# Attention feeding an MLP on one core: weights fetched earlier, less work in the first phase, and the last stores on two queues

## The chip, the core and the metric

The kernel runs on one core of a Trainium2 chip. The core has TensorE (matrix products, written to the accumulation memory PSUM), VectorE, ScalarE and GpSimd (elementwise work), and 16 DMA engines that move data between the chip's memory and the on-chip memory SBUF. SyncE (SP in the profile) issues nearly all DMAs here. The metric is the device time of one execution in microseconds, lower is better.

## The reference

Eight batches of eight heads of attention, with a head dimension of 64. 512 local queries attend to the keys at most 32 positions away and to 32 global keys; 32 global queries attend to all 544 keys. The result, 8 x 544 = 4352 rows of 512, goes through an MLP with a hidden width of 2048.

```python
s_g = scale * q_g @ k_all.T;  out_g = softmax(s_g) @ v_all
s_ll = where(|i - j| <= 32, scale * q_l @ k_l.T, -1e9);  s_lg = scale * q_l @ k_g.T
out_l = softmax(concat(s_lg, s_ll)) @ concat(v_g, v_l)
x = concat(out_g, out_l).transpose(0, 2, 1, 3).reshape(4352, 512)
h = x @ w_in;  out = (h * sigmoid(h)) @ w_out
```

## The kernel before

**Two jobs, one stream of TensorE work.** The attention runs in 128 steps, k = 0 to 127: batch b, a tile c of 128 query rows, a pair of heads pr. Four steps make a tile of x, and 34 tiles (32 local ones, 2 that gather the global queries) make the MLP's 12 blocks: ten of three tiles, two of two (`SIZES`). The first phase is the attention of block 0, steps 0 to 11, with the scores of steps 12 and 13. Then the MLP runs block by block, each with 16 slices f of the hidden width: `first_layer` makes h (12 matmuls), ScalarE and VectorE make gh and gl of it, and `second_layer` adds nine matmuls into the block's outputs (a value is carried as a rounded part and a rest, so each product is three). While block n runs, `fill` slips the attention of block n + 1 between its matmuls.

**A step.** `st_load` fetches raw (queries and keys), `st_scores` makes the scores on TensorE (L357), adds mask and maximum on VectorE (L364), takes the exponential on ScalarE (L368), and scales both halves by the reciprocal of the sum (L372 on ScalarE, L376 on VectorE; for k from 12 to 27 the second is on ScalarE too). `st_turn` transposes the result on TensorE for k below 12 (L404, copied by ScalarE at L406), later steps go over `st_halves` (GpSimd), `st_away` and `st_back` (two DMAs). `st_out` multiplies by v (L437); for k = 4 to 11 it first issues `WARMS[2]` matmuls of zeros into the same bank. The global queries have loads of their own (`g_load`, L234), scores (L259) and a softmax.

**Weights.** A slice f of the weights comes in two halves, w_in's and w_out's, as 8-byte numbers. `fetch_weights(f, half)` issues the DMA of one half (512 KB, L198) into a home that is free by then; `join_weights` makes 4-byte numbers of one half, in order (ScalarE L214, VectorE L216 and L217); `split_weights(f)` makes the rounded part and the rest of a whole slice (ScalarE L226, VectorE L227). In block 0, before slice f, the loop at the end splits slice f + 1, joins up to slice f + 2, and fetches what is not yet fetched of (f + 5, 0) and the half that goes with it.

**Who sets the order.** Everything in the attention is put on a list with a time in units of steps (`put`), and the list, sorted, is the program. `FIRSTW` says how many half slices are fetched at which step, `JOINS` and `SPLITS` at which times the first slices are joined and split. DMAs on SP, the weights' operations and the masks are kept in program order; TensorE's order is the program's; the other instructions of ScalarE and VectorE are ordered by a planner when the program is built. A load that needs a buffer waits on SP until the buffer's last reader is done, and what is queued behind it waits too: raw has two buffers after step 8.

**The end.** After the last block's last slice, ScalarE scales each output tile (L627) and the stores go out: the last block's second tile holds the global rows of four batches and has four stores, on SP; its first tile has one, on ScalarE's queue.

Of the kernel before, what the change touches and what calls it, by code (L numbers as in the profile page):

```python
# [9 lines left out]
F32 = mybir.dt.float32  # L10
# [5 lines left out]
AF = mybir.ActivationFunctionType  # L16
ALU = mybir.AluOpType
# [4 lines left out]
P = 128  # L22
# [3 lines left out]
W = 224  # L26
HALO = 32
SKV = SG + SL
DM, DFF = H * D, 2048
# [9 lines left out]
SIZES = (3,) * 10 + (2, 2)  # L39
# [4 lines left out]
KP = 12  # L44
WHOLE = 9
WARM = 288
WARMS = (14, 8, 3)
SINGLE = 12
SCRATCH = 8
FETCH, LOOK = 5, 3  # L50
PLACES = ("ws15", "ws14", "ws13", "klo", "ws14", "ws15", "klo", "qk")
FIRSTW = {4: 2, 5: 2, 6: 1, 7: 1, 8: 1, 9: 1, 10: 1, 11: 1}
JOINS, SPLITS = (9.0, 9.6, 10.2, 10.8, 11.4, 12.0), (12.1, 12.7)

FIRST = dict(load=(-1.2, -1.1, -1.0, 0.1), vload=(1.22, 1.23, 2.22, 2.23), turn=(3.2, 4.0, 4.9, 5.8), out=(4.3, 5.2, 6.1, 7.0),
             gload=(1.2, 1.21, 2.2, 2.21), gscores=(3.4, 4.2, 5.1, 6.0), gsoft=(4.4, 6.2), gturn=(6.9, 8.0),
             late=8.5, then=7.3)
# [12 lines left out]
def attention_moe_kernel(ctx: ExitStack, tc: tile.TileContext, qk0_in, qk_in, v_in, gqk, wts, out):  # L70
# [274 lines left out]
    def st_scores(k, b, c, pr):  # L345
        if k < ND:
            raw = tiles.pop(("raw", k))
        else:
            qk, klo = tiles.pop(("qk", k))
        s = attbank("s", f"s{k}")  # L350
        if k == 0:
            warm(s, WARMS[0])
        ss = [s[:, u * W : (u + 1) * W] for u in range(2)]
        for u in range(2):
            qs, ks = slice(u * P, (u + 1) * P), slice(u * W, (u + 1) * W)
            if k < ND:
                nc.tensor.matmul(ss[u], raw[:, qs], raw[:, QW : QW + W], start=True, stop=True)  # L357
            else:
                nc.tensor.matmul(ss[u], qk[:, qs], qk[:, QW:][:, ks], start=True, stop=False)  # L359
                nc.tensor.matmul(ss[u], qk[:, qs], klo[:, ks], start=False, stop=True)  # L360
        p = probs_tile(k)
        st = small.tile([P, 8], F32, tag="st", name=f"st{k}")
        for u in range(2):
            nc.vector.tensor_tensor_reduce(out=p[:, u, :W], in0=ss[u], in1=mask_of[c],  # L364
                                           scale=-SCALE, scalar=3.0e38, op0=ALU.add, op1=ALU.min,
                                           accum_out=st[:, u : u + 1])
        for u in range(2):
            nc.scalar.activation(p[:, u, :W], p[:, u, :W], AF.Exp, bias=st[:, u : u + 1], scale=-1.0,  # L368
                                 accum_out=st[:, 2 + u : 3 + u])
        nc.vector.tensor_scalar(out=st[:, 4:6], in0=st[:, 2:4], scalar1=1e-9, scalar2=None, op0=ALU.add)  # L370
        nc.vector.reciprocal(out=st[:, 6:8], in_=st[:, 4:6])  # L371
        nc.scalar.activation(p[:, 0, :W], p[:, 0, :W], AF.Copy, scale=st[:, 6:7])  # L372
        if KF <= k < ND:
            nc.scalar.activation(p[:, 1, :W], p[:, 1, :W], AF.Copy, scale=st[:, 7:8])
        else:
            nc.vector.tensor_scalar(out=p[:, 1, :W], in0=p[:, 1, :W], scalar1=st[:, 7:8], scalar2=None,  # L376
                                    op0=ALU.mult)
        tiles["p", k] = p.rearrange("p u j -> p (u j)")
# [113 lines left out]
    def put(when, fn, *a):  # L492
        stream.append((when, fn, a))

    AHEAD = NPR
    for k, (t, b, c, pr) in enumerate(steps):
        a = (k, b, c, pr)
        j = k % NST
        due = dict(DUE)
        if k >= KF:  # L500
            due.update(DMAT)
            due.update({} if pr else DMAT0)
        if k < AHEAD:
            due.update({part: FIRST[part][k] - k for part in ("load", "vload", "turn", "out")})
        elif pr == 0:
            due["vload"] = VLOADS[min(k // NPR, 3)]
        if k == AHEAD:
            for h in range(NPR):
                put(FIRST["gload"][h], g_load, 0, h)
                put(FIRST["gscores"][h], g_scores, 0, h)  # L510
            for hh in range(2):
                put(FIRST["gsoft"][hh], g_soft, 0, hh)
                put(FIRST["gturn"][hh], g_turn, 0, hh)
            put(FIRST["late"], g_late)
            at = FIRST["then"]
            for when in JOINS:
                put(at + when - NPR, join_weights)
            for f, when in enumerate(SPLITS):
                put(at + when - NPR, split_weights, f)
        if j == 0 and b:  # L520
            for hh in range(2):
                put(at + (TURN if b > 1 else TURN1)[hh], g_turn, b, hh)
        for i in range(FIRSTW.get(k, 0)):
            put(at + 0.01, fetch_weights, *divmod(sum(FIRSTW.get(j, 0) for j in range(k)) + i, 2))
        put(at + due["load"], st_load, *a)
        put(at + due["split"], st_split, *a)
        put(at, st_scores, *a)
        if "vload" in due:
            put(at + due["vload"], st_vload, *a)
        if k >= KF:  # L530
            put(at + due["halves"], st_halves, *a)
            put(at + due["away"], st_away, *a)
        put(at + due["turn"], st_turn, *a)
        if k >= KF:
            put(at + due["back"], st_back, *a)
        if k < SINGLE or pr == NPR - 1:
            n = 1 if k < SINGLE else NPR
            put(at + due["out"], st_out, k - n + 1, n, b, c, t)
            marks[t] = at + due["out"]
        if j == NST - 1 and b % 4 == 3:  # L540
            put(marks[t] + 0.001, g_tile, t + 1)
            marks[t + 1] = marks[t] + 0.001
        if b + 1 < B:
            first, every = HEADS if b > 1 else HEADS0
            for h in [h for h in range(NPR) if first + h * every == j]:
                for part, fn in (("load", g_load), ("split", g_split), ("scores", g_scores)):
                    put(at + HEAD[part], fn, b + 1, h)
                if h % 2:
                    put(at + HEAD["soft"], g_soft, b + 1, h // 2)
                at += HEAD["slot"]  # L550
        at += 1.0
# [26 lines left out]
    def out_rows(t):  # L578
        kind, b, c = order[t]
        if kind == "l":  # L580
            return [(0, P, b * SKV + SG + c * P)]
        return [(SG * i, SG, (4 * b + i) * SKV) for i in range(4)]
# [22 lines left out]
    def second_layer(n, f, gh, gl):  # L605
# [14 lines left out]
            if done_ % 3 == 0:  # L620
                fill(1)
        if f == NF - 1:
            done_ = work.tile([P, 3 * DM], F32, tag=f"xh{n % 2}", name=f"o{n}")
            for i in (reversed(range(SIZES[n])) if last else range(SIZES[n])):
                o = outs[n][i]
                sb = done_[:, DM * i : DM * (i + 1)]
                nc.scalar.activation(sb, o, AF.Copy, scale=0.5)  # L627
                for p0, np_, r in out_rows(sum(SIZES[:n]) + i):
                    queue = nc.sync if n == 0 or last and i else nc.scalar
                    queue.dma_start(out=out[r : r + np_, :], in_=sb[p0 : p0 + np_, :])  # L630

    advance(ends[0])
    early.clear()
# [88 lines left out]
```

## Time and profile before

| | us |
|---|---|
| three runs | 975.33, 976.76, 976.23 (median 976.23) |
| the profiled execution | 976.78 |
| its span, first to last instruction | 974.9 |
| TensorE busy | 950.1 |
| VectorE, ScalarE, GpSimd busy | 624.1, 584.1, 201.7 |
| MLP's first matmul at | 48.17 |

The profile is of one execution. Its own time is longer than its span by what lies before the first and after the last instruction (1.88 us). Times in rows are counted from the span's start. PE is TensorE, PEld its weight loads, DVE VectorE, ACT ScalarE, POOL GpSimd, SPq and ACTq the issue of DMAs on SP and ScalarE. A busy time is a union of instructions, which overlap in the engine's pipeline; matmuls' ends are modelled. PEclk 1.00 is the full granted clock.

### The profile page before, as it was taken

Reading aid. Unit: us, or ns where it says so; the run is one execution under the profiler, and the core shown is the slowest. Engines: PE = TensorE matmul, PEld = TensorE weight load, DVE = VectorE, ACT = ScalarE, POOL = GpSimd, SP = SyncE. Lnnn points to the kernel's source line nnn. Section 1 sums busy time; section 2 is a strip of 40 time slices with the busy share of each in tenths; the row PEclk is TensorE's granted clock in tenths of the full one; section 3 lists DMA queues with packets and bytes.
Section 4 is the critical chain, followed back from the end, with each engine's and each line's share of the span. In section 5 each row is a group of like instructions: output and inputs, shape, how many; then the busy total and the mean of one; then the engine's idle time right before and its main releaser. Section 6 shows DMA issues by size and latency. Waiting matters only on the chain.

```text
span 974.9 us, 17433 instructions
## 1 busy us (share of the span) xinstructions
PE 950.1 (97%) x5790; PEld 847.1 (87%) x5790; DVE 624.1 (64%) x1884; ACT 584.1 (60%) x1494; POOL 201.7 (21%) x413
## 2 busy tenths in 40 slices
PE   7889999999999999999999999999999999999998
PEld 5678788898898989989899899989999899989897
DVE  4888976766676677656577567766677566453322
ACT  7978776656656556555566656665575655443332
POOL 2113222122222122112122222212222221120000
PEclk9999999999999999999999999999999999999999
DMA  8799956656575766534756576575666564433000
GB/s 268 244 275 300 288 158 170 179 158 184 160 169 158 198 156 175 167 98 104 188 146 167 148 211 178 137 201 145 169 192 158 154 163 142 126 91 82 1 23 22
DMA packets 189305, 157.32 MB, mean 161 GB/s; under 512 B 128672, under 2 KB 148640, under 8 KB 189216
## 3 DMA queue, kind: packets, MB, share of 16 engines
q1 hardware_dynamic: 184848, 148.35, 56.0%
q10 hardware_dynamic: 4368, 7.87, 2.3%
q8 instruction: 46, 0.75, 0.3%
q14 instruction: 43, 0.35, 0.1%
HBM read 86.44 MB, written 39.32 MB: 129 GB/s over the span
## 4 chain that ended last, share of the span: by engine, by line
PE 69%; DMA 3%; ACT 1%; DVE 1%; issue 1%; POOL 0%; SPq 0%; ACTq 0%; POOLq 0%; DVEq 0%
PE out L618 30%; PE h L591 29%; PE o L437 5%; PE s L359 2%; PE s L360 2%; DMA raw<-in_qk_dram 2%; DMA raw_g<-in_gqk_dram 1%; DMA away<-halves 0%; PE gs L268 0%; PE gt L305 0%; PE gs L269 0%; POOL halves L386 0%; ACT qk L341 0%; SPq L395 0%; DVE qk L343 0%
## 5 line engine op out<-in xcount | busy, mean ns | idle before, releaser
L386 POOL COPY halves<-probs 128x512 uint16<-128x512 uint16 x232 | 152.1, 682 | 490.7 <-ACT probs L372 186.9
L598 ACT ACTIVATE t<-h 128x384 f32<-128x384 f32 (+1 forms) x192 | 90.5, 472 | 160.0 <-PE h L591 145.0
L599 DVE SCALAR_TENSOR_TENSOR t<-t,h 128x384 f32<-128x384 f32 (+1 forms) x192 | 101.7, 529 | 108.1 <-ACT t L598 107.4
L618 PE MATMUL out<-w_hi,gh 128*128 128x512 f32 x544 | 164.8, 401 | 2.7 <-ACT gh L601 2.6
L591 PE MATMUL h<-xh,w_hi 128*128 128x384 f32 (+1 forms) x768 | 160.6, 330 | 4.7 <-ACT w_hi L226 4.0
L618 PE MATMUL out<-w_hi,gl 128*128 128x512 f32 x544 | 161.2, 395 | 0.2 <-DVE gl L602 0.2
L618 PE MATMUL out<-w_lo,gh 128*128 128x512 f32 x544 | 161.1, 394 | 0.0
L591 PE MATMUL h<-xl,w_hi 128*128 128x384 f32 (+1 forms) x768 | 158.2, 327 | 0.0
L591 PE MATMUL h<-xh,w_lo 128*128 128x384 f32 (+1 forms) x768 | 158.2, 327 | 0.0
L368 ACT ACTIVATE probs<-probs,st 128x224 f32<-128x224 f32 x244 | 115.9, 476 | 59.0 <-DVE st L364 58.1
L591 PEld LDWEIGHTS h<-xh,w_hi 128*128 128x128 f32 x768 | 132.7, 188 | 20.6 <-ACT w_hi L226 6.2
L602 DVE TENSOR_TENSOR gl<-t,gh 128x384 fp32r<-128x384 f32 (+1 forms) x192 | 109.6, 571 | 43.6 <-ACT gh L601 39.4
L364 DVE CUSTOM_DVE_ANT_0 probs<-s,mask 128x224 f32<-128x224 f32 x244 | 86.1, 387 | 74.9 <-PE s L360 63.2
L591 PEld LDWEIGHTS h<-xl,w_hi 128*128 128x128 f32 x768 | 132.7, 188 | 0.0
L591 PEld LDWEIGHTS h<-xh,w_lo 128*128 128x128 f32 x768 | 131.3, 188 | 0.3 <-DVE w_lo L227 0.2
L601 ACT CAST gh<-t 128x384 fp32r<-128x384 f32 (+1 forms) x192 | 94.4, 491 | 55.0 <-DVE t L599 54.7
L618 PEld LDWEIGHTS out<-w_hi,gl 128*128 128x128 f32 x544 | 100.3, 188 | 22.6 <-DVE gl L602 1.0
L618 PEld LDWEIGHTS out<-w_lo,gh 128*128 128x128 f32 x544 | 100.5, 188 | 21.6 <-issue 0.6
L618 PEld LDWEIGHTS out<-w_hi,gh 128*128 128x128 f32 x544 | 93.5, 189 | 14.8 <-ACT gh L601 5.6
L341 ACT CAST qk<-raw 128x704 fp32r<-128x704 f32 x100 | 77.7, 777 | 31.7 <-DMA raw<-in_qk_dram 27.8
L342 DVE TENSOR_TENSOR klo<-raw,qk 128x448 fp32r<-128x448 f32 x100 | 64.4, 644 | 34.1 <-ACT qk L341 31.6
L372 ACT ACTIVATE probs<-probs,st 128x224 f32<-128x224 f32 x122 | 58.6, 480 | 34.1 <-DVE st L371 32.2
(92 smaller groups left out, 1071.3 us busy)
## 6 DMA issues: line engine op xcount, KB each, us to landing
raw<-in_qk_dram SPq DMA_DIRECT2D x100, 352.0 KB, 3.4
away<-halves SPq DMA_DIRECT2D x116, 256.0 KB, 2.9
vraw<-in_v_dram SPq DMA_DIRECT2D x30, 512.0 KB, 4.7
raw_w<-in_wts_dram SPq DMA_DIRECT2D x29, 512.0 KB, 6.2
raw_g<-in_gqk_dram SPq DMA_DIRECT2D x32, 304.0 KB, 4.3
out_dram<-o ACTq DMA_DIRECT2D x29, 256.0 KB, 3.7
raw<-in_qk_dram SPq DMA_DIRECT2D x28, 240.0 KB, 4.5
pt<-away SPq DMA_TRANSPOSE x116, 3.3
```

What stands on the lines that cost most here:

```text
L341: nc.scalar.copy(out=qk, in_=raw)
L342: nc.vector.tensor_tensor(out=klo[:, :KW], in0=raw[:, QW:], in1=qk[:, QW:].bitcast(F32), op=ALU.subtract)
L364: nc.vector.tensor_tensor_reduce(out=p[:, u, :W], in0=ss[u], in1=mask_of[c], scale=-SCALE, scalar=3.0e38, op0=ALU.add, op1=ALU.min, accum_ ...
L368: nc.scalar.activation(p[:, u, :W], p[:, u, :W], AF.Exp, bias=st[:, u : u + 1], scale=-1.0, accum_out=st[:, 2 + u : 3 + u])
L372: nc.scalar.activation(p[:, 0, :W], p[:, 0, :W], AF.Copy, scale=st[:, 6:7])
L386: nc.gpsimd.tensor_copy(out=halves[:, :, u], in_=p[:, 2 * P * u : 2 * P * (u + 1)].bitcast(U16).rearrange("p (j h) -> p h j", h=2))
L591: nc.tensor.matmul(h[:, :nt], wt[:, c * P : (c + 1) * P], x[:, c, :nt], start=(i == 0), stop=(i == 3 * NCC - 1))
L598: nc.scalar.activation(t[:, :nt], h[:, :nt], AF.Tanh, scale=0.5)
L599: nc.vector.scalar_tensor_tensor(out=t[:, :nt], in0=t[:, :nt], scalar=1.0, in1=h[:, :nt], op0=ALU.add, op1=ALU.mult)
L601: nc.scalar.copy(out=gh[:, :nt], in_=t[:, :nt])
L602: nc.vector.tensor_tensor(out=gl[:, :nt], in0=t[:, :nt], in1=gh[:, :nt].bitcast(F32), op=ALU.subtract)
L618: nc.tensor.matmul(outs[n][i], g[:, i * P : (i + 1) * P], w, start=(f == 0 and j == 0), stop=(f == NF - 1 and j == 2))
```

## The change

1. Scaling of the first half (L372) for k below 8 (`LEAN`): VectorE instead of ScalarE.
2. One matmul of zeros instead of three ahead of the outputs of steps 4 to 11.
3. `FIRSTW` becomes a list of half slices by step, 18 instead of 10. Of the eight, (5, 0) and (5, 1) were the first that block 0 issued; the other six, (7, 0), (8, 1), (6, 1), (7, 1), (9, 1) and (10, 1), came in its slices f = 1 to 6. The sorted list puts them on SP thus: load of raw 9, (3, 0), (3, 1), raw 10, (4, 0), (4, 1), raw 11, (5, 0), (5, 1), (7, 0), first global load of batch 1, raw 12, (8, 1), (6, 1), (7, 1), second global load, raw 13, (9, 1), (10, 1), third global load, raw 14. Before it was raw 9, (3, 0), raw 10, (3, 1), raw 11, (4, 0), first global load, raw 12, (4, 1), second global load, raw 13, third, raw 14.
4. Four joins and two splits in the first phase instead of six and two; slice 2 is joined by the loop's first turn.
5. At the end the last tile's eviction is cut in two (ScalarE, VectorE), and the fourth store of the global rows goes on ScalarE's queue behind the store of the last tile.

```diff
@@ -44,13 +44,15 @@
 KP = 12
 WHOLE = 9
 WARM = 288
-WARMS = (14, 8, 3)
+WARMS = (14, 8, 1)
+LEAN = 8
 SINGLE = 12
 SCRATCH = 8
 FETCH, LOOK = 5, 3
 PLACES = ("ws15", "ws14", "ws13", "klo", "ws14", "ws15", "klo", "qk")
-FIRSTW = {4: 2, 5: 2, 6: 1, 7: 1, 8: 1, 9: 1, 10: 1, 11: 1}
-JOINS, SPLITS = (9.0, 9.6, 10.2, 10.8, 11.4, 12.0), (12.1, 12.7)
+FIRSTW = {4: ((0, 0), (0, 1)), 5: ((1, 0), (1, 1)), 6: ((2, 0),), 7: ((2, 1),), 8: ((3, 0), (3, 1)),
+          9: ((4, 0), (4, 1)), 10: ((5, 0), (5, 1), (7, 0)), 11: ((8, 1), (6, 1), (7, 1)), 12: ((9, 1), (10, 1))}
+JOINS, SPLITS = (9.0, 9.7, 10.4, 11.1), (11.8, 12.4)
 
 FIRST = dict(load=(-1.2, -1.1, -1.0, 0.1), vload=(1.22, 1.23, 2.22, 2.23), turn=(3.2, 4.0, 4.9, 5.8), out=(4.3, 5.2, 6.1, 7.0),
              gload=(1.2, 1.21, 2.2, 2.21), gscores=(3.4, 4.2, 5.1, 6.0), gsoft=(4.4, 6.2), gturn=(6.9, 8.0),
@@ -369,7 +371,10 @@
                                  accum_out=st[:, 2 + u : 3 + u])
         nc.vector.tensor_scalar(out=st[:, 4:6], in0=st[:, 2:4], scalar1=1e-9, scalar2=None, op0=ALU.add)
         nc.vector.reciprocal(out=st[:, 6:8], in_=st[:, 4:6])
-        nc.scalar.activation(p[:, 0, :W], p[:, 0, :W], AF.Copy, scale=st[:, 6:7])
+        if k < LEAN:
+            nc.vector.tensor_scalar(out=p[:, 0, :W], in0=p[:, 0, :W], scalar1=st[:, 6:7], scalar2=None, op0=ALU.mult)
+        else:
+            nc.scalar.activation(p[:, 0, :W], p[:, 0, :W], AF.Copy, scale=st[:, 6:7])
         if KF <= k < ND:
             nc.scalar.activation(p[:, 1, :W], p[:, 1, :W], AF.Copy, scale=st[:, 7:8])
         else:
@@ -520,8 +525,8 @@
         if j == 0 and b:
             for hh in range(2):
                 put(at + (TURN if b > 1 else TURN1)[hh], g_turn, b, hh)
-        for i in range(FIRSTW.get(k, 0)):
-            put(at + 0.01, fetch_weights, *divmod(sum(FIRSTW.get(j, 0) for j in range(k)) + i, 2))
+        for f, half in FIRSTW.get(k, ()):
+            put(at + 0.01, fetch_weights, f, half)
         put(at + due["load"], st_load, *a)
         put(at + due["split"], st_split, *a)
         put(at, st_scores, *a)
@@ -620,14 +625,22 @@
             if done_ % 3 == 0:
                 fill(1)
         if f == NF - 1:
-            done_ = work.tile([P, 3 * DM], F32, tag=f"xh{n % 2}", name=f"o{n}")
+            late, done_ = [], work.tile([P, 3 * DM], F32, tag=f"xh{n % 2}", name=f"o{n}")
             for i in (reversed(range(SIZES[n])) if last else range(SIZES[n])):
                 o = outs[n][i]
                 sb = done_[:, DM * i : DM * (i + 1)]
-                nc.scalar.activation(sb, o, AF.Copy, scale=0.5)
-                for p0, np_, r in out_rows(sum(SIZES[:n]) + i):
+                cut = DM // 2 if last and i == 0 else DM
+                nc.scalar.activation(sb[:, :cut], o[:, :cut], AF.Copy, scale=0.5)
+                if cut < DM:
+                    nc.vector.tensor_scalar(out=sb[:, cut:], in0=o[:, cut:], scalar1=0.5, scalar2=None, op0=ALU.mult)
+                for j, (p0, np_, r) in enumerate(out_rows(sum(SIZES[:n]) + i)):
                     queue = nc.sync if n == 0 or last and i else nc.scalar
-                    queue.dma_start(out=out[r : r + np_, :], in_=sb[p0 : p0 + np_, :])
+                    if last and j == 3:
+                        late.append((r, np_, sb[p0 : p0 + np_, :]))
+                    else:
+                        queue.dma_start(out=out[r : r + np_, :], in_=sb[p0 : p0 + np_, :])
+            for r, np_, sb in late:
+                nc.scalar.dma_start(out=out[r : r + np_, :], in_=sb)
 
     advance(ends[0])
     early.clear()
```

## Rows read from the trace of the kernel before

**Rows 1.** The page: busy time of the engines, and the chain of work that ended last by engine.

```profile
PE 950.1 (97%) x5790; PEld 847.1 (87%) x5790; DVE 624.1 (64%) x1884; ACT 584.1 (60%) x1494; POOL 201.7 (21%) x413
...
PE 69%; DMA 3%; ACT 1%; DVE 1%; issue 1%; POOL 0%; SPq 0%; ACTq 0%; POOLq 0%; DVEq 0%
```

**Rows 2.** Busy time by stage. A row has the stretch, its length, for each engine busy us and number of instructions, TensorE's granted clock, the DMA engines' mean share, and GB/s.

```profile
core 0: us, PE busy (x) PEld busy (x) DVE busy (x) ACT busy (x) POOL busy (x), PEclk, DMA share, GB/s
...
10.00:22.00 12.00, 9.49 (x81) 6.28 (x81) 6.04 (x26) 11.42 (x35) 0.81 (x4) 1.00 0.98 309
22.00:32.00 10.00, 9.75 (x84) 7.88 (x85) 6.63 (x35) 8.51 (x28) 1.59 (x7) 1.00 1.04 388
32.00:48.20 16.20, 13.49 (x104) 9.35 (x102) 14.60 (x56) 15.98 (x46) 1.52 (x5) 1.00 0.58 179
48.20:60.00 11.80, 11.08 (x59) 9.57 (x58) 9.34 (x30) 10.54 (x29) 2.35 (x4) 1.00 0.80 254
60.00:75.00 15.00, 12.70 (x61) 9.97 (x59) 11.74 (x32) 10.58 (x26) 1.75 (x4) 1.00 1.13 291
...
90.00:110.00 20.00, 17.06 (x84) 14.57 (x83) 17.49 (x51) 15.81 (x41) 3.85 (x6) 1.00 0.99 300
110.00:140.00 30.00, 28.59 (x183) 25.09 (x183) 27.75 (x77) 23.84 (x63) 7.74 (x15) 1.00 0.75 195
```

**Rows 3.** TensorE's waits from 0 to 140 us: what waited for what, us in total, times, longest.

```profile
PE h L591 <- ACT w_hi L226: 4.0, 4, 1.4
PE gt L305 <- DVE pg L290: 2.5, 2, 1.3
PE s L357 <- DMA raw<-in_qk_dram: 2.2, 2, 1.1
...
PE h L591 <- ACT xh L444: 0.7, 1, 0.7
```

**Rows 4.** The timeline of TensorE at the end of the first phase: start, us, line, operation, count. 32.27 is the scores of step 9, 34.63 of step 10, 47.47 of step 13; 40.75 and 45.56 are the first two global scores of batch 1.

```profile
28.33 0.53 PE L105 MATMUL o<-zeros 128*128 128x288 bf16 x3
28.79 0.71 PE L437 MATMUL o<-pt,vsecond 128*64 128x160 f32 x8
...
32.27 0.92 PE L357 MATMUL s<-raw 128*128 128x224 f32 x4
...
34.63 0.92 PE L357 MATMUL s<-raw 128*128 128x224 f32 x4
...
40.75 0.68 PE L259 MATMUL gs<-raw_g 128*64 128x272 f32 x4
...
45.56 0.68 PE L259 MATMUL gs<-raw_g 128*64 128x272 f32 x4
...
47.47 1.02 PE L357 MATMUL s<-raw 128*128 128x224 f32 x4
48.17 0.85 PE L591 MATMUL h<-xh,w_hi 128*128 128x384 f32 x3
```

**Rows 5.** Groups of instructions in the first 48.2 us: line, engine, operation, count, busy us, mean ns of one, idle time before them.

```profile
L217 DVE SCALAR_TENSOR_TENSOR w<-w,raw_w 128x512 uint32<-128x512 uint32 x6 | 4.2, 698 | 0.3
L214 ACT ACTIVATE w<-raw_w 128x512 f32<-128x512 f32 x6 | 4.1, 681 | 0.0
...
L372 ACT ACTIVATE probs<-probs,st 128x224 f32<-128x224 f32 x6 | 2.8, 473 | 0.5 <-DVE st L371 0.5
...
L216 DVE TENSOR_SCALAR raw_w<-raw_w 128x512 uint32<-128x512 uint32 x6 | 2.5, 420 | 0.0
...
L376 DVE TENSOR_SCALAR probs<-probs,st 128x224 f32<-128x224 f32 x6 | 2.0, 334 | 0.1
```

**Rows 6.** DMA issues with KB and us from issue to landing, first from 23.7 to 24.5 us (raw 9, issued at 23.77, and a slice's half, issued at 24.15), then from 28.5 to 29.3 us (raw 10, at 28.52, and a half, at 28.89).

```profile
raw_w<-in_wts_dram SPq DMA_DIRECT2D x1, 512.0 KB, 8.3
raw<-in_qk_dram SPq DMA_DIRECT2D x1, 240.0 KB, 7.4
...
raw_w<-in_wts_dram SPq DMA_DIRECT2D x1, 512.0 KB, 5.4
raw<-in_qk_dram SPq DMA_DIRECT2D x1, 240.0 KB, 4.5
```

**Rows 7.** The timeline of SP: issue of the last half slice of the first phase, and of the second global load.

```profile
39.64 0.43 SPq L198 DMA_DIRECT2D raw_w<-in_wts_dram  x1
41.47 0.33 SPq L234 DMA_DIRECT2D raw_g<-in_gqk_dram  x1
```

**Rows 8.** TensorE's timeline: the two scores that waited for their load (the wait in brackets). Then SP's waits from 55 to 75 us.

```profile
65.39 1.02 PE L357 MATMUL s<-raw 128*128 128x224 f32 x4 [1.02 <-DMA raw<-in_qk_dram]
...
71.75 1.02 PE L357 MATMUL s<-raw 128*128 128x224 f32 x4 [1.14 <-DMA raw<-in_qk_dram]
...
SPq L395 <- DMA away<-halves: 7.1, 2, 4.5
```

**Rows 9.** The end: the timeline's evictions and stores, and the stores' time to landing, shortest, median and longest.

```profile
969.97 1.29 ACT L627 ACTIVATE o<-out 128x512 f32<-128x512 f32 x2 [1.06 <-PE out L618]
...
970.60 1.75 SPq L630 DMA_DIRECT2D out_dram<-o  x4
...
DMA to landing us min/median/max: 1.6/2.0/2.2
```

## The prediction

> **What bounds the kernel now.** I read the page's busy list and chain first [rows 1]: TensorE is busy for 97% of the span and holds 69% of the chain, so in most of the kernel a shorter job on another engine is worth nothing. Then the table by stage [rows 2], to see where TensorE is not full: TensorE is below 9 tenths from 10 to 22 and 32 to 48 us (phase one: the attention of three tiles) and from 60 to 75 and 90 to 110 (block 0 of the MLP, while weights are still fetched and converted). The change touches these stretches and the last stores. Then the list of TensorE's waits up to 140 us [rows 3], of which four kinds matter here: the weight casts (4.0), the global softmax (2.5), the raw loads (2.2) and the xh copy (0.7). The table also shows what competes in phase one: ScalarE is busy 15.98 of 16.20 us from 32 to 48.2, VectorE 14.60, and the DMA engines, full (1.04) at 388 GB/s from 22 to 32, fall to 0.58 and 179 GB/s after [rows 2]. So it is first TensorE and the DMA engines that are full (22 to 32 us), then ScalarE (32 to 48 us).
>
> **Lighter ScalarE.** For k below 8 the scaling of the first half goes from ScalarE to VectorE: eight instructions of 473 ns [rows 5], which overlap by about 0.1 us, so some 3 us off ScalarE, and eight of 334 ns, 2.7 us, onto VectorE. Four of them lie between 10 and 22 us, where ScalarE is busy 11.42 of 12.00 us and VectorE 6.04 [rows 2]: ScalarE's chain to the two global softmaxes, for which TensorE waits 2.5 us [rows 3], is shorter by three or four of them. I take 1.2 us (bounds 0 and 1.9). The other four lie at 22 to 32 us, where TensorE is full and they only allow the next gain.
>
> **Fewer warm matmuls.** Eight groups fall from three to one. Three took 0.46 us from start to start of what follows (28.33 to 28.79 [rows 4]), so each group loses 0.3 us at most. The step was 2.36 us long (32.27 to 34.63 [rows 4]) with TensorE full; up to k = 10 four groups are on that path: 1.0 us (bounds 0.8 and 1.2). The later groups stand in a stretch that ScalarE limits and are worth nothing.
>
> **One slice joined later.** Two of six half-slice joins leave phase one: on ScalarE 2 x 0.68 = 1.4 us, on VectorE 2 x (0.42 + 0.70) = 2.2 us [rows 5]. From 32 to 48 us that is worth 1.5 us (bounds 0.7 and 2.2). They come back at the head of block 0. Cover there: VectorE was busy 9.34 of 11.80 us between 48 and 60 [rows 2], 2.5 us free; without that cover they cost 2.2 us. Sum so far: the MLP would start 1.2 + 1.0 + 1.5 = 3.7 us sooner, if the loads came in time.
>
> **Six more half slices in phase one.** They don't come in time, I think. All loads go through SP's queue, and the four whose landing I read land in the order of issue: raw 9, issued at 23.77, after 7.4 us, at 31.2; the slice behind it at 32.5; raw 10, issued at 28.52, at 33.0; the slice behind that, issued at 28.89, at 34.3 [rows 6]. Up to raw 9 the change leaves that order as it is. Scores 9 started at 32.27 [rows 4], 1.1 us after their load, and the gains above pull them 2.0 us forward: they wait. Raw 10 now has one half slice more ahead of it, some 1.3 us, and lands at 34.3, for scores that started at 34.63 [rows 4]: the whole gain is gone at that point. Behind it, as the changed table orders the queue: two half slices, raw 11, three, the first global load, raw 12, three, the second global load, raw 13, two. From raw 9 to the second global load that is ten half slices (5.24 MB), three raws (0.74) and two globals (0.62), 6.6 MB. The full stage moved 388 GB/s [rows 2]; the landings from raw 9 to the last slice, 1.29 MB in 3.1 us, make it 417 [rows 6]. So 6.6 MB take 15.8 to 17.0 us, and the second global load lands at 47.0 to 48.2, the first (4.5 MB) at 41.9 to 42.7. Before, the global scores started at 40.75 and 45.56 and the MLP at 48.17, 2.6 us after the second [rows 4]; that load was issued at 41.47 with nothing behind the slice of 39.64 [rows 7]. With 0.4 us less of warm matmuls and waits between them, the MLP starts at 49.2 to 50.4; I take 1.5 us later than before. TensorE would wait some 4 us for the first global load and some 3 for the second. Bounds: 3.7 us sooner if the loads are hidden anyway; 6.6 later if the queue moves only the 309 GB/s of 10 to 22 us [rows 2] (21.4 us for the 6.6 MB). I keep to the middle since the load is the same mix as that of 22 to 32 us.
>
> The Trainium skill (HBM Reference, Specifications) gives a core that streams alone about 425 GB/s. The trace's fullest stage shows 388 [rows 2]. By the page the 6.6 MB would take 15.5 us, the MLP would start 0.7 us later than before, and the sum would come out 0.8 us lower.
>
> **What block 0 gets back.** Up to f = 6 it issues eight half slices fewer. Both waits for raw loads, 1.02 and 1.14 us [rows 8], stand where SP held 7.1 us for the away planes to land [rows 8] with weight slices ahead of them; with the slices gone I take all 2.2 us back (bounds 0 and 2.5). The 0.7 us for xh [rows 3] goes too: ScalarE is idle while TensorE waits for the globals. For the same reason the joined slice costs nothing, and of the 4.0 us of waits for weight casts [rows 3] I take 0.9 (bounds 0 and 2): the first of them follows on the raw waits, the others are ScalarE's own order and stay.
>
> **The tail.** The last eviction took about 0.6 us (two in 1.29 [rows 9]); halved it gives 0.2. SP issues three stores instead of four, 1.75 us for four [rows 9]; the fourth goes behind ScalarE's store. Landing takes 2.0 us [rows 9], so the end moves from the fourth store to the third: 0.25 us (bounds 0 and 0.5).
>
> **Sum.** + 1.5 - 0.7 - 2.2 - 0.9 - 0.25 = -2.55 us. The profiled execution was 976.78 with a span of 974.9, so 974.2; against the median of 976.23, which is 0.55 lower, it is 973.7. The MLP's other eleven blocks keep their instructions and I move nothing in them.
>
> **The rivals.** (a) *The weights are hidden anyway*: the queue isn't full, or moves more than 388 GB/s, and phase one keeps its 3.7 us. For it: 0.58 of the DMA engines' time was used from 32 to 48 us [rows 2]. Against: the free part of that stretch, 16.2 us x (388 - 179) GB/s = 3.4 MB, is hardly more than the 3.15 MB of six half slices, and shrinks when the phase does. Time: 976.2 - 3.7 - 0.7 - 2.2 - 0.9 - 0.25 = 968.5. (b) *The queue moves 309 GB/s*: the MLP starts 6.6 us later, so 976.2 + 6.6 - 0.7 - 2.2 - 0.9 - 0.25 = 978.8. For it: the 12 us in which the first weights came [rows 2]. Against: the 10 us after them, with the same mix. (c) *VectorE takes over the raw waits' place*, the case on the other side: it has 2.2 us of joins more in block 0, the two raw waits turn into waits for casts, and the end is 976.2 + 1.5 + 2.2 - 0.7 - 0.25 = 979.0. It decides where VectorE is full; it was busy 27.75 of 30.00 us from 110 to 140, but only 11.74 of 15.00 from 60 to 75 [rows 2]. (d) *TensorE's clock falls* in the new waits of phase one. In the trace the granted clock was 1.00, that is 2.4 GHz, in every stage [rows 2], and no wait there was over 1.4 us [rows 3]; the new ones are 3 to 4 us with no warm matmul in them. At 1.2 GHz some 4 us of matmuls of the end of phase one would take 4 us more: 977.7. The Trainium skill (TensorE: Matmul & The Clock Gate, Part 1) says that an idle TensorE falls back to 1.2 GHz and is let up again by activity; no stretch of this trace shows such a fall between the first matmul and the last.
>
> **How the numbers follow.** A change of 0.2%, 1.95 us, is about what a measurement of this kernel can tell from none. My forecast has 0.50; its own range, from the bounds of the cast waits and of the rate, is 971.5 to 975.8, so that 0.36 of it is faster and 0.14 the same. (a) has 0.22, all faster; (b) 0.10, of it 0.03 the same; (c) 0.10, of it 0.02 the same; (d) 0.08, of it 0.05 the same. Faster 0.36 + 0.22 = 0.58, same 0.14 + 0.03 + 0.02 + 0.05 = 0.24, slower 0.18. The range is 968.5 to 978.8: it leaves out about 0.09 of (a), 0.05 of (b) and 0.06 of (c), 0.2 in all.
>
> **What would show it.** Right: in the changed profile TensorE waits for raw 9 or 10, and for both global loads, on the DMA; DMA share about 1.0 from 32 to 48 us; the MLP's first matmul at 49 to 50.5 us; no wait for a raw load after 60 us; the last store landing some 2.2 us after its issue on either queue. Wrong: the first MLP matmul before 47 us and no wait for a load (rival a), or after 52 (b); cast waits above 4.0 us in all (c); a granted clock below 1.00 between 40 and 55 us (d).

## The result: slower, 982.1 us against 976.55

The median of the changed kernel is 982.1 us (978.05 to 986.02, 15 executions), that of the kernel before, run beside it, 976.55 (975.33 to 981.13, 15 executions). The ratio is 1.0054, with an interval of 1.0042 to 1.0066: slower by half a per cent, where 973.7 was forecast. The profiled execution took 980.06 us with a span of 977.9, so some 2 us of the median's excess are in no row below.

The table by stage of the changed kernel answers to [rows 2]. Columns: stretch, its length, busy us and instructions of PE, PEld, DVE, ACT and POOL, granted clock, DMA share, GB/s.

```profile
22.00:32.00 10.00, 9.38 (x80) 7.21 (x80) 7.57 (x39) 7.45 (x27) 1.57 (x7) 1.00 1.04 391
32.00:48.20 16.20, 9.95 (x67) 6.85 (x67) 11.30 (x46) 12.79 (x38) 1.94 (x4) 0.87 0.95 339
48.20:60.00 11.80, 11.50 (x52) 8.92 (x53) 7.71 (x22) 8.61 (x23) 2.57 (x5) 0.75 0.47 149
...
75.00:90.00 15.00, 15.00 (x89) 13.81 (x89) 12.96 (x33) 12.22 (x33) 3.73 (x6) 0.90 0.78 230
```

In three of these stretches the granted clock is clearly below 1.00; in [rows 2] it is 1.00 in every stage. From 32 to 48.2 us the DMA engines are now full (0.95 against 0.58) and ScalarE is not (12.79 us against 15.98): the bound of that stretch has moved from ScalarE to the loads. TensorE's waits up to 140 us, against [rows 3] (us in all, times, longest):

```profile
PE h L596 <- ACT w_hi L228: 5.1, 4, 2.2
PE gs L261 <- DMA raw_g<-in_gqk_dram: 3.4, 2, 1.9
...
PE s L359 <- DMA raw<-in_qk_dram: 0.6, 1, 0.6
```

The two waits for raw loads in block 0 [rows 8] and the wait for xh are gone; two waits for global loads are new; the waits for weight casts rose from 4.0 to 5.1 us. The 0.6 us for a raw load is step 11's (raw 11), in the first phase. TensorE's timeline (start, us, line, operation, count, in brackets the idle time before and what ended it):

```profile
42.36 0.68 PE L261 MATMUL gs<-raw_g 128*64 128x272 f32 x4 [1.55 <-DMA raw_g<-in_gqk_dram]
...
43.84 1.77 PE L359 MATMUL s<-raw 128*128 128x224 f32 x4
...
48.35 1.18 PE L261 MATMUL gs<-raw_g 128*64 128x272 f32 x4 [1.89 <-DMA raw_g<-in_gqk_dram]
...
52.32 1.79 PE L596 MATMUL h<-xh,w_hi 128*128 128x384 f32 x4
...
56.16 0.85 PE L596 MATMUL h<-xl,w_hi 128*128 128x384 f32 x4
...
73.63 0.97 PE L596 MATMUL h<-xh,w_hi 128*128 128x384 f32 x4 [2.15 <-ACT w_hi L228]
...
75.50 1.48 PE L596 MATMUL h<-xh,w_lo 128*128 128x384 f32 x4
```

The four scores matmuls that took 1.02 us at 47.47 in [rows 4] take 1.77 here at 43.84, and four h matmuls take 1.79 us at 52.32 and 0.85 at 56.16. The next table puts the clock beside what TensorE did just before it fell.

```profile
40.00:44.00 4.00, 2.30 (x18) 1.35 (x19) 2.79 (x6) 3.46 (x9) 0.17 (x1) 0.99 0.97 365
44.00:54.00 10.00, 8.11 (x30) 5.87 (x31) 5.04 (x21) 6.17 (x18) 1.47 (x4) 0.50 0.71 245
...
72.00:74.50 2.50, 0.87 (x5) 0.88 (x6) 2.18 (x7) 2.50 (x6) 0.00 (x0) 1.00 0.88 322
75.00:78.00 3.00, 3.00 (x12) 2.89 (x10) 2.79 (x5) 2.10 (x5) 1.84 (x2) 0.50 0.90 179
```

From 44 to 54 us, and from 75 to 78, TensorE ran at 0.50, that is 1.2 GHz. Ahead of the first fall it had been busy 2.30 of 4.00 us, ahead of the second 0.87 of 2.50, behind a wait for a cast. The MLP starts at 52.32 us, 4.1 later than before; its first matmul of block 1 is 3.3 us later, the last one of the kernel 3.0.

The end, against [rows 9]: the evictions and stores, and then the landing of the store issued last (KB, us from issue to landing).

```profile
972.97 1.07 ACT L633 ACTIVATE o<-out 128x512 f32<-128x512 f32 x2 [1.05 <-PE out L623]
...
973.60 1.28 SPq L641 DMA_DIRECT2D out_dram<-o  x3
973.67 0.35 ACTq L643 DMA_DIRECT2D out_dram<-o  x1
974.08 0.42 DVE L635 TENSOR_SCALAR o<-out 128x256 f32<-128x256 f32 x1 [1.70 <-ACT o L633]
974.54 0.35 ACTq L641 DMA_DIRECT2D out_dram<-o  x1
```

```profile
out_dram<-o ACTq DMA_DIRECT2D x1, 256.0 KB, 2.4
```

SP's last store no longer ends the kernel; the one on ScalarE's queue does, issued behind VectorE's half of the eviction. And that half begins at 974.08, when ScalarE is done with its own: the two halves run one after the other, not side by side.

### The profile page after: what moved, and what is told of

It is laid out like the page before. It is cut to its first block, busy times and chain, and to the rows that moved or that the text cites. A ratio compares the mean times of both kernels' runs of the same rounds, so it can differ in the third digit from the quotient of the medians.

```text
span 977.9 us, 17406 instructions
## 1 busy us (share of the span) xinstructions
PE 952.4 (97%) x5774; PEld 849.7 (87%) x5774; DVE 627.5 (64%) x1893; ACT 581.0 (59%) x1486; POOL 200.4 (20%) x413
## 4 chain that ended last, share of the span: by engine, by line
PE 86%; DVE 5%; ACT 4%; DMA 3%; issue 1%; SPq 0%; POOL 0%; ACTq 0%; DVEq 0%
PE h L596 36%; PE out L623 35%; PE o L442 6%; DMA raw_g<-in_gqk_dram 2%; PE s L361 2%; PE s L362 2%; PE s L359 1%; DVE w L219 1%; DMA raw<-in_qk_dram 1%; DVE w_lo L229 1%; DVE raw_w L218 1%; PE gt L307 1%; DVE probs L366 1%; PE gs L270 1%; ACT probs L370 1%
```

## The experiments

Four chips, each with the kernel before run beside the others: its medians were 978.89 us (the first four runs below), 978.69 (the next four), 979.58 (three) and 977.25 (the last). Ratios are to the kernel before on the same chip. No run leaves out any of the computation.

**The fetches, taken out of the change and done alone.** First the changed kernel with the old table:

```
-FIRSTW = {... 8: ((3, 0), (3, 1)), 9: ((4, 0), (4, 1)), 10: ((5, 0), (5, 1), (7, 0)), ...}
+FIRSTW = {... 8: ((3, 0),), 9: ((3, 1),), 10: ((4, 0),), 11: ((4, 1),)}
```

> The changed kernel with the fetch table of before (10 half slices in phase one, in the order of before); lighter ScalarE, one warm matmul, four joins and the new stores stay. Theory Q (the eight half slices fill the DMA queue in phase one, the global loads come late, TensorE waits and its clock falls): no wait for a load before the MLP, granted clock 1.00 up to 60 us, the MLP's first matmul at 44.5 to 46.5 us, two waits for raw loads in block 0 again; 971 to 975 us, ratio to before 0.995 to 0.999. Rival J (the slice joined later overloads block 0, or the lighter phase one loses the clock by itself): 976.5 us or more, and the clock falls or the waits for weight casts exceed 5 us.

Measured: 977.31 us, ratio 0.9988 (0.9974 to 1.0002). Its timeline of TensorE:

```profile
43.39 0.68 PE L261 MATMUL gs<-raw_g 128*64 128x272 f32 x4 [0.76 <-DMA raw_g<-in_gqk_dram]
...
45.57 1.02 PE L596 MATMUL h<-xh,w_hi 128*128 128x384 f32 x4
```

The MLP starts 2.6 us sooner than before, in the range expected, and the clock stays at 1.00. The ratio is in the range expected too; the time is not (971 to 975), but the kernel before is 2.3 us slower on this chip as well. One wait for a load stands ahead of the MLP, 0.8 us, where none was expected, and one for a raw load in block 0, 0.5 us, where two were. Then the kernel before with nothing but the new table:

```
-FIRSTW = {4: 2, 5: 2, 6: 1, 7: 1, 8: 1, 9: 1, 10: 1, 11: 1}
+FIRSTW = {4: ((0, 0), (0, 1)), ..., 12: ((9, 1), (10, 1))}
```

> The kernel before with the new fetch table alone. Theory Q: the first global load lands at about 42.3 us and the second at about 48.3, as in the changed kernel; TensorE waits some 1.5 us for each, the MLP starts at 50 to 52 us, the waits for raw loads after 60 us are gone; 977 to 982 us. Rival J: the fetches cost nothing by themselves, the MLP starts at 48 us and block 0 gains 2 us: 974 to 975 us.

Measured: 981.32 us, ratio 1.0026 (1.0014 to 1.0038).

```profile
42.40 0.68 PE L260 MATMUL gs<-raw_g 128*64 128x272 f32 x4 [1.80 <-DMA raw_g<-in_gqk_dram]
...
49.78 1.18 PE L260 MATMUL gs<-raw_g 128*64 128x272 f32 x4 [2.73 <-DMA raw_g<-in_gqk_dram]
...
54.23 1.04 PE L592 MATMUL h<-xh,w_hi 128*128 128x384 f32 x4
```

The same two waits, the MLP 6.1 us later (54.2 us; 50 to 52 were expected), the clock at half from 44.0 to 54.2 us. So the fetches bring the loss, and the clock falls with three warm matmuls ahead of each output as with one. They also do what they are for: no wait for a raw load is left in block 0, which takes 3.2 us less.

**The clock apart from the loads.** The changed kernel with 16 more matmuls of zeros ahead of the two global scores; no load is taken away or moved:

```
+            if b == 1 and p < 2:
+                warm(s, 16)
```

> The changed kernel with 16 matmuls of zeros before each of the first two global scores of batch 1, where TensorE waits for the load: the loads come as late as before, but TensorE is not idle. Theory Q, its clock part: granted clock 1.00 from 32 to 60 us, the MLP's first matmul at 49.5 to 50.5 us instead of 52.3, 977 to 979.5 us, 2.5 to 4.5 less than the changed kernel. Rival (the clock's fall costs little, the late loads alone make the loss): 981 to 983 us.

Measured: 977.99 us, ratio 0.9992 (0.9979 to 1.0004).

```profile
39.58 2.12 PE L107 MATMUL gs<-zeros 128*128 128x288 bf16 x16
41.91 0.68 PE L263 MATMUL gs<-raw_g 128*64 128x272 f32 x4 [0.20 <-DMA raw_g<-in_gqk_dram]
...
44.68 2.12 PE L107 MATMUL gs<-zeros 128*128 128x288 bf16 x16
47.16 0.68 PE L263 MATMUL gs<-raw_g 128*64 128x272 f32 x4 [0.36 <-DMA raw_g<-in_gqk_dram]
...
49.34 1.03 PE L598 MATMUL h<-xh,w_hi 128*128 128x384 f32 x4
```

No load is spared, zeros fill the time until they land, the clock stays at 1.00 until the last matmul, and the MLP starts at 49.34 us instead of 52.32. That is 3.0 us, but not all of it is the clock: this trace is ahead from its first 16 scores on, where the two kernels are the same. First the changed kernel, then the one with zeros:

```profile
4.41 4.18 PE L359 MATMUL s<-raw 128*128 128x224 f32 x16
```

```profile
4.18 3.54 PE L361 MATMUL s<-raw 128*128 128x224 f32 x16
```

They end at 8.59 and at 7.72 us. Counted from there the clock is worth 2.1 us at the MLP's start, and 0.8 more in the MLP's first twelve matmuls, which take 3.15 us instead of 2.31. This run shows the clock as a cause and not as a companion of the waits: only work without a result was added. The other executions agree. Each has its mean granted clock on record: 0.990 to 0.997 in the 15 of the changed kernel (0.992 in the profiled one), 0.997 to 1.000 in the 12 with zeros, as in the kernel before on their chip. And the version with the old fetches has 977.31 us on that chip: with the clock held, the eight half slices more cost 0.7 us, which the intervals don't tell from nothing.

**Is it the global loads' place alone?** The half slices of steps 10 to 12 put behind the global load of their step:

```
-            put(at + 0.01, fetch_weights, f, half)
+            put(at + (0.45 if k >= 10 else 0.01), fetch_weights, f, half)
```

> The changed kernel with the half slices of steps 10, 11 and 12 put on the queue behind the global load of the same step instead of ahead of it; the same 18 half slices in phase one. Theory Q in its narrow form (what counts is what stands ahead of the global loads): the global loads land before 40 and 44 us, the waits for them go, the MLP starts at 47 to 49 us, clock 1.00, 974 to 978 us. Theory Q in its wide form (what counts is the bytes ahead of the last load that the MLP needs, raw 13): the wait moves to the raw loads 12 and 13, the MLP starts at 50 us or later, 979 to 983 us.

Measured: 982.14 us, ratio 1.0039 (1.0024 to 1.0054).

```profile
43.23 1.02 PE L359 MATMUL s<-raw 128*128 128x224 f32 x4 [1.95 <-DMA raw<-in_qk_dram]
...
49.90 1.86 PE L359 MATMUL s<-raw 128*128 128x224 f32 x4 [2.73 <-DMA raw<-in_qk_dram]
51.26 1.79 PE L596 MATMUL h<-xh,w_hi 128*128 128x384 f32 x4
```

The wide form holds: the waits move to the next loads in the queue. What counts here are the bytes ahead of phase one's last load, wherever a single load stands among them; the clock falls again, from 44.8 to 55.1 us.

**The half slices behind phase one's last load, and the joins.** Three runs on one chip. The changed kernel with the old fetches and also the old joins:

```
-JOINS, SPLITS = (9.0, 9.7, 10.4, 11.1), (11.8, 12.4)
+JOINS, SPLITS = (9.0, 9.6, 10.2, 10.8, 11.4, 12.0), (12.1, 12.7)
```

> The changed kernel with the fetch table and the join and split times of before: six joins in phase one. Lighter ScalarE, one warm matmul and the new stores stay. Theory L (the slice joined late is paid back in block 0, where VectorE is near full): the MLP starts some 1.5 us later than with four joins (46 to 47.5 us), but block 0 takes 1.5 to 2.5 us less, so that it is no slower than the kernel with the old table and four joins; 0.996 to 0.9985 of before. Rival: the late join is free, then this is 1 to 1.5 us slower than that kernel: 0.999 to 1.001.

Measured: 982.97 us, ratio 1.0047 (1.0029 to 1.0064): neither theory had this; it is taken up below. The old fetches with four half slices added at step 12, behind raw 13:

```
+           ..., 12: ((5, 0), (5, 1), (7, 0), (7, 1))}
```

> The changed kernel with the fetch table of before and four half slices more, (5, 0), (5, 1), (7, 0) and (7, 1), put at step 12, where the queue has them behind raw 13, the last load that the MLP's first matmul waits for. Theory Q: they cost phase one nothing (first matmul of the MLP at 45 to 46.5 us, clock 1.00), and relieve the queue between 48 and 65 us; 0.996 to 0.9985 of before, equal to or up to 1.5 us less than the old table with four joins. Rival (any fetch more in phase one costs): the third global load or raw 14 come late and it is slower than before.

Measured: 983.03 us, ratio 1.0045 (1.0031 to 1.0060). The rival was right: the MLP starts sooner (46.27 us), but the third global load now stands behind the slices. And both edits together:

> The two last edits together: six joins in phase one and four half slices more behind raw 13; lighter ScalarE, one warm matmul, the new stores. If both theories hold this is the fastest: MLP's start at 46 to 47.5 us, block 0 some 3 us shorter than before, 0.9945 to 0.9975 of before. If the gains are taken back by later waits: 0.998 to 1.000.

Measured: 982.2 us, ratio 1.0039 (1.0024 to 1.0053), off both. The third global score in the one and in the other:

```profile
53.95 0.80 PE L261 MATMUL gs<-raw_g 128*64 128x272 f32 x4 [3.19 <-DMA raw_g<-in_gqk_dram]
```

```profile
55.12 1.17 PE L261 MATMUL gs<-raw_g 128*64 128x272 f32 x4 [3.49 <-DMA raw_g<-in_gqk_dram]
```

There was no place for four more half slices at this point of SP's queue: the wait goes to the next load behind them, and the clock falls behind it (0.86 and 0.73 in the mean from 48.2 to 60 us).

**The kernel before, profiled once more.** A run to see how far two traces of one kernel differ.

> The kernel before, profiled once more, on this chip: how much the waits in the later blocks differ between two traces of one kernel. If they are the program's own, TensorE waits again for gh only about 0.3 us between 600 and 700 us, and the blocks start where they did within 0.5 us; if they vary from run to run or chip to chip, a wait of 1 us or more stands there as in the changed kernels, and differences of 1 to 3 us between traces after block 0 mean nothing.

Measured: 979.1 us, one execution. Its waits, first up to 140 us, then from 140 us to the end:

```profile
PE s L357 <- DMA raw<-in_qk_dram: 1.0, 1, 1.0
```

```profile
PE out L618 <- ACT gh L601: 4.2, 5, 1.8
```

The first trace has 2.2 us of raw waits [rows 3] and, after 140 us, 1.8 of the second kind. Block 1 starts 2.2 us sooner than in the first trace and the end comes 2.4 later. Shifts of 2 to 4 us behind block 0 are therefore no evidence in a single trace. The MLP starts 1.1 us sooner (47.08), and all of that is there when the first 16 scores end, here in the first and in the second trace:

```profile
4.40 4.47 PE L357 MATMUL s<-raw 128*128 128x224 f32 x16
```

```profile
4.29 3.51 PE L357 MATMUL s<-raw 128*128 128x224 f32 x16
```

From that end, 8.87 and 7.80 us, to the MLP it is 39.30 and 39.28 us. Counted so, the MLP comes 4.4 us later than before in the changed kernel (not 4.1) and 2.3 later with zeros (not 1.2); with the old fetches it comes 1.5 sooner (not 2.6; 1.7 in a second run of that version, below).

**The rest of the change, in parts.** First the joins and splits of the change alone, in the kernel before.

> The kernel before with nothing changed but the joins and splits of the change: four half-slice joins in phase one and two later, splits at 11.8 and 12.4. Theory S (what counts is the order on SP: with the splits earlier the away plane is ready sooner, so SP issues the weight slices behind it some 3 to 4 us sooner after the MLP's start, and the raw loads of block 0 come in time): MLP start 1 to 2 us sooner than in the kernel before, waits for raw loads in block 0 below 0.8 us, ratio 0.997 to 0.999. Rival L (the late joins are only paid later, on VectorE in block 0): MLP start as in S, but waits for casts in block 0 above 5 us and a ratio of 0.9995 to 1.002.

Measured: 977.15 us, ratio 0.9987 (0.9973 to 1.0000). Beside it the changed kernel with twelve half slices instead of eighteen (the expectation counts the sixteen ahead of the second global load), and that with the old table a second time:

```
+FIRSTW = {... 8: ((3, 0), (3, 1)), 9: ((4, 0), (4, 1)), 10: ((5, 0),), 11: ((5, 1),)}
```

> The changed kernel with twelve half slices fetched in phase one instead of sixteen (before: ten), none behind raw 12 and only one ahead of the second global load. Theory C (waits for casts, not for the weights' arrival, limit block 0, so slices fetched sooner have nothing to give there): MLP first matmul at 45.5 to 47.0 us, waits for casts in the first 140 us 4.5 to 5.2 us in all as in the changed kernel with the old fetch table, ratio 0.998 to 1.001. Rival W (two more half slices spare block 0 a wait): waits for casts below 4.0 us, ratio 0.995 to 0.9975.

> The changed kernel with the fetch table of the kernel before, a second time, beside the two runs of this job and on their chip: the same theories as the first time. If the gain of the first time (ratio 0.9988, interval up to 1.0002) is one, it is 0.997 to 0.999 here; if it is the scatter of a chip, 0.9995 to 1.002. In the profile: MLP first matmul at 45 to 46 us, granted clock 1.00 from 30 to 60 us, waits for casts 4.5 to 5.2 us.

Measured: 979.47 us for twelve, ratio 1.0003 (0.9988 to 1.0017), and 977.36 for the old table, ratio 0.9981 (0.9968 to 0.9994). Last, the lighter phase one alone in the kernel before (eight scalings moved, one warm matmul for three):

> The kernel before with the lighter first phase alone: eight scalings moved to VectorE and one warm matmul in place of three; the joins, the fetch table and the stores are those before. Theory G (the gain of phase one is given back in block 0, since SP's queue behind the away plane stays as late as it was): MLP first matmul at 45.5 to 47 us, waits for raw loads up to 140 us of 2 to 4 us (2.2 in the kernel before), ratio 1.000 to 1.005. Rival F (the terms of the sum hold): MLP start 1.5 to 2.2 us sooner and kept, waits for raw loads at most 2.2 us, ratio 0.9975 to 0.999.

Measured: 981.41 us, ratio 1.0036 (1.0020 to 1.0053). Why the lighter phase loses alone and the joins win is seen on GpSimd and SP at the head of block 0: the copy for batch 0's away planes, then their DMA and the slices behind it. GpSimd's timeline in the kernel before, with the lighter phase alone, and with the new joins alone:

```profile
49.09 1.18 POOL L386 COPY halves<-probs 128x512 uint16<-128x512 uint16 x2 [1.06 <-ACT probs L372]
```

```profile
49.56 1.38 POOL L390 COPY halves<-probs 128x512 uint16<-128x512 uint16 x2 [4.27 <-ACT probs L376]
```

```profile
46.17 1.17 POOL L386 COPY halves<-probs 128x512 uint16<-128x512 uint16 x2 [0.35 <-ACT probs L372]
```

SP's timeline with the lighter phase alone, and with the new joins alone:

```profile
50.97 0.35 SPq L395 DMA_DIRECT2D away<-halves  x1
51.37 0.92 SPq L199 DMA_DIRECT2D raw_w<-in_wts_dram  x2
```

```profile
47.37 0.35 SPq L391 DMA_DIRECT2D away<-halves  x1
47.77 0.95 SPq L198 DMA_DIRECT2D raw_w<-in_wts_dram  x2
```

With six joins, the softmax of step 12 that GpSimd waits for is done at about 49 us (48.0 in the second trace of the kernel before) whether the MLP starts at 48.17 or, as with the lighter phase, at 46.42. SP holds the slices and raw loads behind the away plane until then, so TensorE comes sooner to loads that are no sooner. TensorE's timeline with the lighter phase alone:

```profile
64.89 1.02 PE L358 MATMUL s<-raw 128*128 128x224 f32 x4 [2.34 <-DMA raw<-in_qk_dram]
...
87.34 2.37 PE L441 MATMUL o<-pt,vraw 128*64 128x160 f32 x16 [2.12 <-POOL halves L390]
```

The raw waits are 5.4 us in all (2.2 before, and 2 to 4 expected), and the first of them alone takes more than the 1.8 us that the MLP's start had gained (1.0 counted from the first scores). This execution took 978.76 us, 2.7 less than the median, so the rows show only a part of the loss. With four joins the copy starts at 46.17, the slices are issued 3.6 us sooner, and no wait for a raw load is left up to 140 us: that is theory S, and its ratio is in the range expected. That this order on SP is the reason is read from the traces; no run changed it alone. The run with the old fetches and the six joins shows the same as the lighter phase alone, the second of its late waits too:

```profile
64.92 1.02 PE L359 MATMUL s<-raw 128*128 128x224 f32 x4 [1.85 <-DMA raw<-in_qk_dram]
...
87.78 1.31 PE L442 MATMUL o<-pt,vraw 128*64 128x160 f32 x16 [2.14 <-POOL halves L391]
```

And the raw waits of block 0, which the fetches were to take away, are gone by the joins alone (with twelve half slices three short ones are left, 1.2 us). The waits that stay are those for casts, with twelve half slices and with ten:

```profile
PE h L596 <- ACT w_hi L228: 4.3, 4, 1.6
```

```profile
PE h L596 <- ACT w_hi L228: 4.3, 5, 1.4
```

More fetched weights do nothing for these, as theory C said; with eighteen half slices they are 5.1 us. They go with the joins instead: in the six traces with six joins in phase one they are 2.0 to 4.0 us, in the eight with four 4.2 to 5.1.

## Why the prediction was wrong

**The failing step: a wait of TensorE was priced as its length alone.** The prediction saw the two waits for the global loads, saw that no warm matmul stood in them, and still summed at full clock, with 0.08 for rival (d). The sentence on which that rested, that no wait in [rows 3] was over 1.4 us and the clock 1.00, says nothing of longer waits in a stretch where TensorE has less to do; it was no evidence against a fall. The run with zeros sizes the omission: 2.1 us at the MLP's start and 0.8 in its first matmuls, behind waits of 1.55 and 1.89 us where some 4 and 3 were forecast. Three signs of being wrong came together, the MLP after 52 us (b), cast waits above 4.0 (c) and the clock (d); that the zeros alone take the loss away says that (d) was the one that counted for the time. (d) named the mechanism, with a price of 4 us and a place that are near (44.0 to 54.2 us), but set it on top of a block 0 that gives back 3.8. The Trainium skill (TensorE: Matmul & The Clock Gate, Part 1) says that the clock is lowered by default and that activity raises it; the trace agrees, with 0.50 behind a stretch in which TensorE was busy 2.30 of 4.00 us, and 1.00 with zeros in the same waits.

**Six more half slices: the landings right.** Raw 10 landed at 33.84 us (34.3 forecast), the first global load at 42.31 (41.9 to 42.7), the second at 48.30 (47.0 to 48.2). The scores of steps 9 and 10 did not wait for their loads, as they were to; those of step 11 did, 0.55 us. With the clock held the MLP starts at 49.34, 1.2 us later than before, or 2.3 counted from the first scores (1.5 forecast). The 6.6 MB from raw 9's landing at 30.61 us on took 17.7 us, 373 GB/s, less than the 391 of the stage before and far from the 309 of rival (b). The rate of the Trainium skill (HBM Reference, Specifications), about 425 GB/s for a core that streams alone, stays further off than the row: no stage in the table was above 391 GB/s.

**What block 0 gets back: 0.8 us, not 3.8.** That is 94.21 us from the MLP's first matmul to block 1's, 95.06 before; two traces of one kernel differ by 1 to 2 us in it (93.92 in the second trace before), so 0.8 may be nothing, but 3.8 it is not. The raw waits (2.2) and the xh wait (0.7) went, as forecast. The cast waits were to fall by 0.9 and rose by 1.1, and one of them, 2.15 us, stands ahead of the second fall of the clock, 3.4 us at half for matmuls that fill it: 1.7 us. In the run with zeros, where the clock held, block 0 gave back 0.6 us all the same: cast waits 4.2 us and waits for gh 2.3, 6.5 together where the kernel before had 4.8. Other waits, all of them on ScalarE, take what the loads give; it is the course of rival (c), with ScalarE's casts in the place of VectorE's joins. The term that failed here, as far as the traces tell, is the joined slice, which was to cost nothing: with six joins, in the kernel before, the same fetches left 3.7 us of cast waits and block 0 gave back 3.2.

**The lighter phase: smaller than summed, and its worth wrong.** 3.7 us sooner were summed if the loads came in time; with the old fetches it is 2.6, or 1.5 to 1.7 counted from the first scores, with 0.8 us of waits for loads among it. And the parts don't add: alone, the lighter phase costs 0.36% and the new joins gain 0.13%; together, with the new stores, they gain 0.12 to 0.19% (0.9988 and 0.9981). The prediction costed the late join as work put off (2.2 us of VectorE); its worth, by the traces, is that batch 0's softmax, and so SP's queue behind the away plane, gets free sooner.

**The tail: 0.25 us forecast, next to nothing measured.** The step that failed is the eviction cut in two, which was to be shorter by 0.2: VectorE's half waited for ScalarE's, and the two evictions end 1.53 us after their start instead of 1.29. The three stores on SP take 1.28 us instead of 1.75, but the store on ScalarE's queue is issued only at 974.54 and takes 2.4 us to land. From the start of the last evictions to the last landing it is 3.95 us; before, 969.97 to 973.95 in the trace, 3.98.

**What stays open.** The three single effects (0.36% slower, 0.13% faster, 0.26% slower for the fetches) sum to 0.49%, near the 0.54% measured, but that is chance: the first two don't add, and the fetches cost 0.26% in the kernel before and 0.66 to 0.73% on top of the rest of the change. Why, is open. The clock's second fall is in the changed kernel's trace and not in that of the fetches alone; the mean clocks of the other executions (0.990 to 0.997, and 0.992 to 0.998 with the fetches alone) say that nearly all lost some clock, not where. The version with zeros was not run beside the changed kernel on one chip, so the two are compared by their ratios to the kernel before (0.9992 and 1.0054); it is 4.1 us below the half slices put behind the global loads, which ran beside it. The tail was not tried alone, nor the moved scalings without the fewer warm matmuls.

The version that beats both kernels is the change without its fetches: 0.9988 and 0.9981 on two chips, the second's interval below 1. The new joins alone do about as well (0.9987, interval up to 1.0000).

## What to carry to other kernels

A new wait of TensorE can cost its length and what its clock does behind it: where a prefetch makes TensorE wait in a stretch that is already thin, sum the matmuls behind the wait at half the clock too, or put work of zeros in the wait. In the one queue for all loads here, a prefetch was paid by the next load that somebody waited for, and moving it by a place moved the wait and not the bytes. Before weights are fetched sooner, look at what their users wait for: here, by the traces, the raw loads were held up by SP's wait for one small plane, and the casts by ScalarE's order.

## What the runs showed of the hardware

The clock fell behind waits of 1.55 and 2.15 us, short against the 3 and 4 us for which the prediction had feared it, with TensorE busy more than half of the time ahead of the first. The length of a wait does not decide it: with the lighter phase alone the clock stays at 1.00 behind the wait of 2.34 us that ends at 64.89 and is at half from 87.4 to 90.8, behind one of 2.12; with the old fetches and the six joins it is at half from 66.2 to 69.6, behind the 1.85 us that end at 64.92, and stays at 1.00 behind the 2.14 that end at 87.78. It fell without any change too, in the second trace of the kernel before (columns as in the tables by stage):

```profile
475.20:478.60 3.40, 3.40 (x11) 2.75 (x10) 1.11 (x2) 2.43 (x5) 0.12 (x1) 0.50 0.68 217
```

Ahead of it TensorE had waited 1.8 us for one gh and been busy 5.00 of 7.00 us. So a single execution of the kernel before can lose up to 1.7 us in the middle of the MLP (an estimate, half of the 3.40). And 16 matmuls of zeros of 288 columns, 2.12 us, ahead of each of the two late loads held the clock where it had fallen without them.
